# Tile 0 takes the norm's factor at the sums of MoE 1, smaller slice groups, low weight parts stored in DRAM, and a new hand-written order

## The chip, the cores and the metric

The kernel runs on one core of one Trainium2 chip. The metric is the device time of one execution in microseconds (us); the time of a kernel is the median of several executions. All four compute engines take part: TensorE (PE in the profile), VectorE (DVE), ScalarE (ACT) and GpSimd (POOL); SP only issues transfers. Each engine works through its own instructions strictly in the order in which the program lists them.

## The reference, cut to what matters

Three stages follow each other: a linear attention with a decay for each head, a gated MLP (MoE 1) on the normalised attention output, and a second gated MLP without a norm or a silu (MoE 2).

```python
# attention: B=2, H=8 heads, S=768 positions, D=64, blocks of 64 (the kernel uses chunks of 128)
intra = (q @ k.T) * Dmask              # decay lam**(i-j) inside a block
out   = intra @ v + (q * lam_pow) @ kv_state
kv_state = lam_block * kv_state + (k * rev_pow).T @ v
# x: 1536 tokens x 512
rms = sqrt(mean(x * x, -1) + 1e-6);  xn = x / rms * rms_g
g = xn @ w_gate;  y = (silu(g) * (xn @ w_val)) @ w_out     # MoE 1, d_ff = 1536
a = y @ w_a;      z = (a * (y @ w_b)) @ w_out2             # MoE 2, d_ff = 1536
```

## The kernel before

**Number format.** Every large product is done on numbers split into a high part and a low part (fp32r), as hi·hi + hi·lo + lo·hi. So a weight tile has a `whi` (a cast on ACT, L312, word `hi`) and a `wlo` (a subtraction on DVE, L317, word `lo`), and an activation tile has an `xhi` and an `xlo`. The weights arrive as integers of 64 bits and are turned into floats by two copies on ACT (L260, L264, word `c`) and seven operations on DVE (L282 to L301, word `k`) for each of 24 slices.

**Tiling.** The 1536 tokens are three tiles of 512 tokens. Each tile holds two chunks of 128 positions for both batches: tile 0 has chunks 0 and 1, tile 1 chunks 2 and 3, tile 2 chunks 4 and 5. d_ff is cut into 12 slices of 128 in each MoE. A plain step (`G` gate, `V` value, `O` output) takes one slice and one tile through 12 + 12 + 12 matmuls of 128x512. A pair step takes one slice and tiles 1 and 2 together through seven products `P` of 6 matmuls (a Strassen scheme on halves) and two outputs `Q` of 12. A pair slice needs its own sums of weight blocks (`ws` on DVE), their splits (`uh` on ACT, `ul` on DVE) and more element-wise work on both engines (`ps`, `pa`, `pm`, `sl`, `ph`, `pl`).

**Groups.** `GROUPS` cuts the slices: in MoE 1 slices 0 to 5 run plain for all three tiles and slices 6 to 11 run plain for tile 0 and as pairs for tiles 1 and 2. In MoE 2 all 12 slices are plain for tile 0 and pairs for the rest, in two groups. At the end of each group the sums in PSUM are added to SBUF (`E`, `e`: copies on ACT L572 for the first group, additions on DVE L574 for the others).

**Attention.** For chunk c and batch b: `S.b.c` scores (L358), `am` mask with the decay table `dt` on DVE (L369), `kd` and `qd` the decays of k and q on POOL (L337, L349), `U` the new state (L378), `I` and `X` the output (L393, L408). The state is decayed on POOL (`sd`, L418) and added to on DVE (`sa`, L428).

**The norm.** `sq` squares on ACT (L440); `rd` reduces four blocks of squares to one on DVE (L444); `R` sums over the partitions by matmuls with ones (L454), four of them where `rd` isn't done and one where it is; `ms` (DVE, L461), `rr` the power -1/2 on POOL (L468), `dg` a diagonal matrix (DVE, L473), `N` a matmul that spreads the factors over the partitions (L478), `nx` multiplies the attention output by factor and g (DVE, L484), `xh` and `xl` split it (ACT L492, DVE L498). In the kernel before `rd` is done for chunks 2 to 5. The gate of a tile can start when its two chunks have gone through all of this.

**Order.** Nothing is scheduled automatically. `PROGRAM` lists words such as `G.0` (gate of step 0) or `am.1.3.1` (mask, batch 1, chunk 3, half 1), and each word issues its instructions at once, so the list is the order on every engine. The transfers are words too: `l.i` a stage of weights of 512 KB on the SP queue (L234), `A` and `L` the pieces of q, k and v (L224), `Z` and `D` write the table of decays to DRAM and read it back spread over the partitions (L776, L753, L758). `W` issues dummy matmuls (L767) that keep PE active before there is work.

Of the kernel before, what the change touches and what calls it, by code (L numbers as in the profile page):

```python
# [38 lines left out]
GROUPS = [(0, 6), (6, 12)]  # L39

SLOTS, OUT_SLOTS = 7, 10

# [826 lines left out]
```

## Time and profile before

| | |
|---|---|
| time, median of 3 runs | 656.45 us (655.95 to 657.09) |
| profiled execution | 655.5 us, span 653.8 us |
| PE busy | 638.9 us (98%) |
| DVE busy | 520.1 us (80%) |
| ACT busy | 405.0 us (62%) |
| POOL busy | 39.7 us (6%) |
| mean granted clock of PE | 0.992 |

A profile comes from one execution. An engine's busy time is the time in which one of its instructions was running. A wait is named after what ended it: `[1.67 <-DVE nrm L473]` is idle time of 1.67 us that ended when that instruction of DVE did. The granted clock is 1.00 at 2.4 GHz and 0.50 at 1.2 GHz.

### The profile page before, as it was taken

The numbers are of one execution on the slowest core, as the hardware profiler recorded it, in microseconds if no ns is written. First come the engines' busy times: TensorE is split into PE (matmuls) and PEld (weight loads), VectorE is DVE, ScalarE is ACT, GpSimd is POOL, SyncE is SP. The second block draws the span as 40 slices with busy tenths as digits, with TensorE's granted clock in tenths as the row PEclk, the third lists the DMA queues.
The fourth block names the chain that finished last, engine by engine and source line by source line (L and its number), as shares of the span: only waits on it lengthen the run. The fifth ranks groups of instructions, "written<-read, shape, count | busy, mean of one in ns | idle before, by whom it ended". The sixth has DMA issues, their size and how long they took to land.

```text
span 653.8 us, 8719 instructions
## 1 busy us (share of the span) xinstructions
PE 638.9 (98%) x3304; PEld 517.5 (79%) x3306; DVE 520.1 (80%) x889; ACT 405.0 (62%) x642; POOL 39.7 (6%) x43
## 2 busy tenths in 40 slices
PE   9989999999999999999999999999999999999997
PEld 4767777787888888878887888888887888888876
DVE  4789999655579999889999988857968688776664
ACT  2878853332599884379888655665559873444441
POOL 1533122110000000000000000000000000000000
PEclk9969999999999999999999999999999999999999
DMA  8945641110036520013233120020023220100011
GB/s 262 378 156 188 226 161 65 65 65 1 4 127 194 162 96 1 1 36 126 66 99 127 64 65 1 0 66 33 1 96 97 67 63 1 65 1 0 2 64 65
DMA packets 16506, 54.84 MB, mean 84 GB/s; under 512 B 1864, under 2 KB 3408, under 8 KB 15440
## 3 DMA queue, kind: packets, MB, share of 16 engines
q1 hardware_dynamic: 15600, 47.99, 22.2%
q10 hardware_dynamic: 864, 6.29, 2.7%
q8 instruction: 26, 0.43, 0.3%
q14 instruction: 16, 0.13, 0.1%
HBM read 51.12 MB, written 3.15 MB: 83 GB/s over the span
## 4 chain that ended last, share of the span: by engine, by line
PE 86%; DVE 9%; DMA 2%; SPq 1%; ACT 1%; issue 0%; POOL 0%; ACTq 0%; DVEq 0%; POOLq 0%
PE acc L562 27%; PE at L706 15%; PE gv L706 11%; PE gv L514 6%; PE gv L518 6%; PE gv L515 5%; PE at L515 3%; PE at L514 3%; PE at L518 3%; DMA att<-att_dram 1%; DVE sums L574 1%; PE at L393 1%; PE at L358 1%; DVE wlo L317 1%; PE at L408 1%; DVE hh L301 1%
## 5 line engine op out<-in xcount | busy, mean ns | idle before, releaser
L260 ACT COPY hh<-stage 128x1024 uint8<-128x1024 uint8 x72 | 75.2, 1045 | 6.7 <-DMA stage<-w_dram 6.5
L514 PE MATMUL gv<-xhi,whi 128*128 128x512 f32 x192 | 76.7, 399 | 0.0
L317 DVE TENSOR_TENSOR wlo<-w,whi 128x512 fp32r<-128x512 f32 (+1 forms) x108 | 69.7, 654 | 7.8 <-ACT whi L312 7.8
L515 PE MATMUL gv<-xlo,whi 128*128 128x512 f32 x192 | 74.9, 390 | 0.0
L312 ACT CAST whi<-w 128x512 fp32r<-128x512 f32 (+1 forms) x108 | 60.5, 585 | 14.1 <-PE acc L562 5.6
L537 ACT CAST hhi<-s 128x512 fp32r<-128x512 f32 x36 | 22.4, 622 | 50.7 <-DVE s L533 49.1
L317 DVE TENSOR_TENSOR wlo<-o,whi 128x512 fp32r<-128x512 f32 x72 | 50.5, 705 | 3.5 <-ACT whi L312 3.4
L518 PE MATMUL gv<-xhi,wlo 128*128 128x512 f32 x192 | 51.6, 391 | 1.4 <-DVE wlo L317 1.4
L264 ACT COPY w<-stage 128x1024 uint16<-128x1024 uint16 x48 | 50.2, 1045 | 0.0
L312 ACT CAST whi<-o 128x512 fp32r<-128x512 f32 x72 | 44.2, 620 | 8.9 <-PE acc L562 4.3
L518 PEld LDWEIGHTS gv<-xhi,wlo 128*128 128x128 f32 x192 | 35.9, 188 | 9.7 <-DVE wlo L317 2.2
L562 PE MATMUL acc<-hlo,whi 128*128 128x512 f32 x144 | 42.1, 392 | 0.9 <-DVE hlo L541 0.6
L562 PE MATMUL acc<-whi,hlo 128*128 128x512 f32 x144 | 42.9, 391 | 0.0
L514 PEld LDWEIGHTS gv<-xhi,whi 128*128 128x128 f32 x192 | 36.1, 188 | 8.4 <-issue 0.9
L562 PE MATMUL acc<-hhi,whi 128*128 128x512 f32 x144 | 42.5, 395 | 0.2
L562 PE MATMUL acc<-whi,hhi 128*128 128x512 f32 x144 | 42.2, 392 | 0.1
L562 PE MATMUL acc<-wlo,hhi 128*128 128x512 f32 x144 | 41.8, 390 | 0.0
L515 PEld LDWEIGHTS gv<-xlo,whi 128*128 128x128 f32 x192 | 36.1, 188 | 7.0
L562 PE MATMUL acc<-hhi,wlo 128*128 128x512 f32 x144 | 41.5, 390 | 0.0
L706 PE MATMUL at<-T,whi 128*128 128x512 f32 x144 | 38.5, 389 | 0.0
L514 PE MATMUL at<-xhi,whi 128*128 128x512 f32 x96 | 37.3, 389 | 0.0
L515 PE MATMUL at<-xlo,whi 128*128 128x512 f32 x96 | 37.3, 389 | 0.0
(167 smaller groups left out, 1405.0 us busy)
## 6 DMA issues: line engine op xcount, KB each, us to landing
stage<-w_dram SPq DMA_DIRECT2D x72, 512.0 KB, 3.4
att<-att_dram ACTq DMA_DIRECT2D x6, 1024.0 KB, 4.8
att<-att_dram SPq DMA_DIRECT2D x6, 512.0 KB, 5.6
out_dram<-sums SPq DMA_DIRECT2D x12, 256.0 KB, 2.1
att<-att_dram SPq DMA_DIRECT2D x2, 1024.0 KB, 8.3
att<-att_dram SPq DMA_DIRECT2D x4, 256.0 KB, 9.6
dt<-ext_d SPq DMA_DIRECT2D x2, 256.0 KB, 4.7
p<-ext_d SPq DMA_DIRECT2D x2, 128.0 KB, 4.6
```

Of the source, the lines that this page charges most:

```text
L260: nc.scalar.copy(hh_t[i][:, into].bitcast(U8).rearrange("p (n e) -> p n e", e=2), st.rearrange("p (n e) -> p n e", e=8)[:, :, 3:5],)
L264: nc.scalar.copy(home(i, slice(place, place + 1)).bitcast(U16).rearrange("p (n e) -> p n e", e=2), st.bitcast(U16).rearrange("p (n e) -> p ...
L301: nc.vector.tensor_tensor(out=hh, in0=hh, in1=t, op=ALU.bitwise_or)
L312: nc.scalar.copy(whi[key], src)
L317: nc.vector.tensor_sub(wlo[key], src, whi[key].bitcast(F32))
L358: nc.tensor.matmul(ps[r][:, a * C : (a + 1) * C], lhsT=t[r * D : (r + 1) * D, 1, a * C : (a + 1) * C], rhs=t[r * D : (r + 1) * D, 0, a * C ...
L514: nc.tensor.matmul(ps, lhsT=w, rhs=xhi[t][:, k, :], start=k == 0, stop=False)
L515: nc.tensor.matmul(ps, lhsT=w, rhs=xlo[t][:, k, :], start=False, stop=False)
L518: nc.tensor.matmul(ps, lhsT=w, rhs=xhi[t][:, k, :], start=False, stop=k == KD - 1)
L537: nc.scalar.copy(h_t[g][0], s_t[g])
L562: nc.tensor.matmul(acc[j], lhsT=lhsT, rhs=rhs, start=first and n == 0, stop=last and n == 2)
L706: nc.tensor.matmul(ps, lhsT=w[:, k * 128 : (k + 1) * 128], rhs=x[:, k, :], start=first and n == 0, stop=n == len(todo) - 1, skip_group_che ...
```

## The change

1. `GROUPS` of MoE 1 becomes slices 0 to 2, 3 to 6 and 7 to 11. Only slices 0 to 2 run plain for all tiles; slices 3 to 11 are pairs for tiles 1 and 2. Plain steps go from 36 to 30 (the steps of tile 1 in slices 0 to 2 are `G.3` to `G.5`, those of tile 2 `G.6` to `G.8`, tile 0 goes on with `G.9`), pair slices from 18 to 21.
2. Tile 0 goes into MoE 1 as attention output times g, without the factor 1/rms. `xs` (ACT, four pieces of 128x128) and `xd` (DVE, four pieces) write its high and low part straight from PSUM. The factors are kept in a row `rv` (`rv`, ACT copy of the spread factors); the gate is multiplied by it ahead of the silu (`gs`, DVE, 12 steps), and the finished sums of MoE 1 are multiplied by it (`sr`, four DVE operations). `xg`, `nx`, `xh` and `xl` go away for chunks 0 and 1.
3. The state's decay leaves POOL (`sd` goes away); `sa` does decay and addition in four DVE operations of 128x64.
4. `rd` is done for chunks 4 and 5 only; `R` of chunks 2 and 3 is four matmuls again.
5. The low parts of slices 0 to 2 are computed once for tile 0, stored to DRAM (`ls`, 9 transfers of 256 KB) and loaded again for tiles 1 and 2 (`lr`, 18 transfers), all on the SP queue, in place of 18 subtractions.
6. `Z` and `D` are issued from ACT's queue. `l.0` is the first large transfer on SP's queue, with chunk 0 of q and k behind it.
7. The dummy matmuls go from 46 to 37, all ahead of `S.0.0`; before, 34 stood ahead of it and four times 3 between it and `G.0`.
8. The conversion of slice 1 is done in three parts (28 more `k` instructions). All words stand in a new order.

```diff
-GROUPS = [(0, 6), (6, 12)]
-SLOTS, OUT_SLOTS = 7, 10
-LAST_ATT = 11
+GROUPS = [[(0, 3), (3, 7), (7, 12)], [(0, 6), (6, 12)]]
+SLOTS, OUT_SLOTS = 7, 9
+def beside(i, t):
+    return i < GROUPS[0][0][1] and t < 2 or i < GROUPS[0][1][1] and t == 0
...
-    A.0.0.0 W.8.1 W.14 W.3.1 W.7.1 W.2.1 S.0.0 W.3.1 A.0.0.2 l.0 g Z A.1.0.0 A.1.0.2 D.0 D.1 A.0.1.0 A.1.1.3
+    W.14 W.8.1 W.7.1 W.2.1 l.0 A.1.0.0 A.1.1.0 A.0.1.0 A.0.0.0 A.0.0.2 A.1.1.3 A.1.0.2 g A.1.1.2 W.3.1 W.3.1 S.0.0
...
+    def lo_store(g, part):
+        nc.sync.dma_start(out=wlo_d[g * 3 + part], in_=wlo[g, part].bitcast(F32))
+    def lo_load(g, part):
+        wlo[g, part] = spool.tile([128, 512], F32R, tag="wlo", name="wlo")
+        nc.sync.dma_start(out=wlo[g, part].bitcast(F32), in_=wlo_d[steps[g][0] * 3 + part])
...
-    def state_decay(b, c):
-        nc.gpsimd.tensor_tensor(
-            out=st_t[b], in0=st_t[b], in1=p1[:, :, C - 1 : C].to_broadcast([128, NP, D]), op=ALU.mult
-        )
...
-            nc.vector.tensor_add(st_t[b], st_t[b], pu)
+            for a in range(NP):
+                nc.vector.scalar_tensor_tensor(
+                    out=st_t[b][:, a], in0=st_t[b][:, a], scalar=p1[:, a, C - 1 : C], in1=pu[:, a], op0=ALU.mult, op1=ALU.add
+                )
...
+    def att_hi(b, c):
+        hi = xtiles(0)[0]
+        for k in range(KD):
+            nc.scalar.mul(hi[:, k, c * 256 + b * C : c * 256 + (b + 1) * C], px_t[b, c][:, k * C : (k + 1) * C], g_sb[:, k, :])
+    def att_lo(b, c):
+        hi, lo = xtiles(0)
+        for k in range(KD):
+            some = (slice(None), k, slice(c * 256 + b * C, c * 256 + (b + 1) * C))
+            nc.vector.scalar_tensor_tensor(
+                out=lo[some], in0=px_t[b, c][:, k * C : (k + 1) * C], scalar=g_sb[:, k, :], in1=hi[some].bitcast(F32),
+                op0=ALU.mult, op1=ALU.subtract,
+            )
...
+    def factors(c):
+        nc.scalar.copy(rv[:, c * 256 : (c + 1) * 256], pr_t[c][:, 0:256])
...
+    def gate_factors(g):
+        s_t[g] = hpool.tile([128, 512], F32, tag="s", name="s")
+        nc.vector.tensor_tensor(out=s_t[g], in0=pg_t[g], in1=rv, op=ALU.mult)
...
+    def sum_factors(j):
+        nc.vector.tensor_tensor(out=sums[0][:, j, :], in0=sums[0][:, j, :], in1=rv, op=ALU.mult)
...
-                nc.sync.dma_start(
+                nc.scalar.dma_start(
                     out=dt[:, r],
...
-        "Z": lambda: nc.sync.dma_start(out=ext_d, in_=ext), "D": decay_tables,
+        "Z": lambda: nc.scalar.dma_start(out=ext_d, in_=ext), "D": decay_tables,
```

Three places show the new order. The first is PE ahead of the first gate `G.0`. Before, between the last matmuls with ones of chunk 1 (L454) and the gate (L514, here its first row) stand the spread of chunk 1's factors (L478), the scores of chunk 2 (L358, one of four pairs of rows shown) and the rest of chunk 2's batch 0:

```order
L454 MATMUL acc_445<-ones,sq 128x1 x4
L478 MATMUL at_472<-nrm,ones 128x128 x2
L358 MATMUL at_486<-att_2_293 128x128
L358 MATMUL at_487<-att_2_293 128x128
...
L378 MATMUL at_509<-att_2_293,kd 64x64 x8
L393 MATMUL at_518<-qd,st 64x128 x8
L408 MATMUL at_518<-am,att_2_293 64x128 x8
L514 MATMUL gv_535<-xhi_414,whi 128x512
```

After, with the names of the changed kernel's lines (L416 inter, L431 output of the attention, L514 spread, L490 matmuls with ones, L381 scores, L553 and L554 the gate, L401 state):

```order
L416 MATMUL acc_399<-spare,st 64x128 x8
L431 MATMUL acc_399<-am,att_1_158 64x128 x8
L514 MATMUL at_420<-nrm,ones 128x128 x2
L490 MATMUL acc_434<-ones,sq 128x1 x4
L381 MATMUL at_443<-att_2_441 128x128
L381 MATMUL at_444<-att_2_441 128x128
...
L553 MATMUL gv_470<-xhi_254,whi 128x512
L554 MATMUL gv_470<-xlo_255,whi 128x512
...
L401 MATMUL at_485<-att_2_441,kd 64x64 x8
L490 MATMUL acc_494<-ones,sq 128x1 x4
L553 MATMUL gv_531<-xhi_254,whi 128x512
```

The spread ahead of the gate is now chunk 0's; `U.0.2` (L401) and the matmuls of `R.1.1` (L490) stand behind the gate, and the spread of chunk 1, `I.0.2` and `X.0.2` behind the value `V.0`, which is the second L553 row.

The second is DVE in the changed kernel at the end of the stretch that leads to the normalisation of chunk 3 (L310 to L299 are the conversion of weights, L497 `ms`, L447 the state, L509 the diagonal, L523 `nx`, L392 the mask of the scores `S.0.4`):

```order
L310 TENSOR_SCALAR t<-t 128x1536
L295 TENSOR_SCALAR o_875<-o_875 128x512
L295 TENSOR_SCALAR w_831<-w_831 128x1024
L314 TENSOR_TENSOR hh<-hh,t 128x1536
L299 SCALAR_TENSOR_TENSOR o_875<-o_875,hh 128x512
L299 SCALAR_TENSOR_TENSOR w_831<-w_831,hh 128x1024
L497 TENSOR_SCALAR ms<-at_1043 128x1
L447 SCALAR_TENSOR_TENSOR st<-st,p_88,at_938 128x64 x4
L509 TENSOR_SCALAR nrm<-ident,rr 128x128 x2
L523 SCALAR_TENSOR_TENSOR spare<-spare,g_sb,at_1057 128x256 x4
```

All of slice 4's conversion stands ahead of `ms.1.3`, and the two words that the norm of chunk 3 needs next stand behind it. On PE the matmuls around it are these (L609 output, L490 `R.1.3`, L514 `N.3`, L381 `S.0.4`):

```order
L609 MATMUL acc_760<-hhi,wlo 128x512
L609 MATMUL acc_760<-hlo,whi 128x512
L490 MATMUL at_1043<-ones,sq 128x1 x4
L514 MATMUL at_1057<-nrm,ones 128x128 x2
L381 MATMUL at_1075<-att_4_833 128x128
L381 MATMUL at_1076<-att_4_833 128x128
```

Nothing else stands on PE between `R.1.3` and `N.3`, nor between `N.3` and `S.0.4`, and the gate of tile 1's first step comes behind the latter.

## Rows read from the trace of the kernel before

**Rows 1.** The page: busy time of PE, share of the span.

```profile
PE 638.9 (98%) x3304; PEld 517.5 (79%) x3306; DVE 520.1 (80%) x889; ACT 405.0 (62%) x642; POOL 39.7 (6%) x43
```

**Rows 2.** Windows by stage: PE, PEld, DVE, ACT, POOL busy, PEclk, DMA share.

```profile
11.40:44.40 33.00, 28.47 (x339) 23.32 (x340) 25.17 (x51) 21.89 (x30) 17.01 (x15) 0.84 0.84 294
31.00:33.70 2.70, 1.21 (x10) 1.03 (x9) 1.94 (x7) 2.45 (x4) 1.19 (x2) 0.94 0.75 293
33.70:43.30 9.60, 7.08 (x54) 5.88 (x56) 8.45 (x17) 7.11 (x9) 3.55 (x3) 0.50 0.55 182
...
44.40:100.00 55.60, 53.18 (x372) 42.19 (x371) 52.60 (x87) 42.40 (x61) 12.28 (x11) 1.00 0.54 182
...
100.00:120.00 20.00, 18.76 (x133) 15.03 (x131) 18.47 (x31) 9.16 (x17) 4.45 (x4) 1.00 0.08 34
120.00:275.00 155.00, 154.69 (x799) 127.16 (x798) 118.36 (x188) 93.27 (x146) 5.03 (x5) 1.00 0.23 75
275.00:390.00 115.00, 113.92 (x500) 93.17 (x499) 107.36 (x188) 92.02 (x146) 0.00 (x0) 1.00 0.26 83
```

**Rows 3.** Timeline of PE up to the first gate: start, duration, instruction, wait.

```profile
11.49 1.16 PE L358 MATMUL at<-att 64*128 64x128 f32 x16
...
18.11 0.69 PE L378 MATMUL acc<-att,kd 128*64 128x64 f32 x16
18.77 1.05 PE L454 MATMUL acc<-ones,sq 128*128 128x1 f32 x8
19.75 1.16 PE L358 MATMUL gv<-att 64*128 64x128 f32 x16
...
23.27 1.09 PE L408 MATMUL acc<-am,att 128*64 128x128 f32 x16 [0.35 <-DMA att<-att_dram]
...
26.50 0.81 PE L767 MATMUL gv<-warm 128*128 128x512 bf16 x3
27.24 0.69 PE L378 MATMUL acc<-att,spare 128*64 128x64 f32 x16
...
34.62 1.22 PE L478 MATMUL at<-nrm,ones 128*128 128x128 f32 x4 [1.67 <-DVE nrm L473]
...
37.69 2.05 PE L358 MATMUL at<-att 64*128 64x128 f32 x14 [1.11 <-DVE spare L484]
...
44.40 0.50 PE L514 MATMUL gv<-xhi,whi 128*128 128x512 f32 x1
```

**Rows 4.** Chain that ended last: start, duration, what.

```profile
33.23 1.03 POOL rr L468
...
35.88 1.67 DVE spare L484 x4
...
281.41 2.72 PE acc L562 x12
```

**Rows 5.** Timeline of DVE while it works without a gap.

```profile
61.52 0.69 DVE L282 TENSOR_SCALAR w<-w 128x1024 uint32<-128x1024 uint32 x1
62.12 0.55 DVE L295 TENSOR_SCALAR t<-t 128x1536 uint16<-128x1536 uint16 x1
62.59 0.69 DVE L317 TENSOR_TENSOR wlo<-w,whi 128x512 fp32r<-128x512 f32 x1
...
64.33 0.95 DVE L301 TENSOR_TENSOR hh<-hh,t 128x1536 uint16<-128x1536 uint16 x1
65.20 0.68 DVE L533 TENSOR_TENSOR s<-s,gv 128x512 f32<-128x512 f32 x1
65.80 0.68 DVE L286 SCALAR_TENSOR_TENSOR o<-o,hh 128x512 f32<-128x512 uint32 x1
66.40 1.22 DVE L286 SCALAR_TENSOR_TENSOR w<-w,hh 128x1024 f32<-128x1024 uint32 x1
67.53 0.48 DVE L473 TENSOR_SCALAR nrm<-ident,rr 128x128 f32<-128x128 f32 x2
```

**Rows 6.** DMA issues of the page: KB each, us from issue to landing.

```profile
out_dram<-sums SPq DMA_DIRECT2D x12, 256.0 KB, 2.1
```

More of the change, by code (lines that the diff above doesn't have):

```diff
@@ L201, in chain_kernel @@
     g_sb = cpool.tile([128, KD, 1], F32, tag="g_sb", name="g_sb")
+    rv = cpool.tile([128, 512], F32, tag="rv", name="rv")
     ones = cpool.tile([128, 128], F32, tag="ones", name="ones")
@@ L323, in split_lo @@
         unit_lo((g, part), third(steps[g][0], part))
+    wlo_d = dpool.tile([GROUPS[0][0][1] * 3, 128, 512], F32, tag="wlo_d", name="wlo_d")
+    def lo_store(g, part):
[3 more added lines that the diff above has]
+        nc.sync.dma_start(out=wlo[g, part].bitcast(F32), in_=wlo_d[steps[g][0] * 3 + part])
     a_t, kd_t, qd_t, st_t, ps_t, pu_t, px_t = {}, {}, {}, {}, {}, {}, {}
@@ L503, in chain_kernel @@
         (m * NF + f, t, f == lo, f == hi - 1)
-        for m in range(2) for lo, hi in GROUPS for t in range(1 if m or lo else len(TILES)) for f in range(lo, hi)
+        for m in range(2) for lo, hi in GROUPS[m] for t in range(1 if m or lo else len(TILES)) for f in range(lo, hi)
     ]
@@ L520, in gate @@
     def gate(g):
-        pg_t[g] = bank("at0" if g > LAST_ATT and g % 2 else "gv0")
+        pg_t[g] = bank("at0" if g % 2 and not beside(*steps[g][:2]) else "gv0")
         proj(pg_t[g], g, 0)
     def value(g):
-        pv_t[g] = bank("at1" if g > LAST_ATT and g % 2 else "gv1")
+        pv_t[g] = bank("at1" if g % 2 and not beside(*steps[g][:2]) else "gv1")
         proj(pv_t[g], g, 1)
+    def gate_factors(g):
+        s_t[g] = hpool.tile([128, 512], F32, tag="s", name="s")
+        nc.vector.tensor_tensor(out=s_t[g], in0=pg_t[g], in1=rv, op=ALU.mult)
     def silu(g):
-        s_t[g] = hpool.tile([128, 512], F32, tag="s", name="s")
-        nc.scalar.activation(s_t[g], pg_t[g], AF.Silu if steps[g][0] < NF else AF.Copy)
+        i, t, _, _ = steps[g]
+        if i < NF and t == 0:
+            nc.scalar.activation(s_t[g], s_t[g], AF.Silu)
+        else:
+            s_t[g] = hpool.tile([128, 512], F32, tag="s", name="s")
+            nc.scalar.activation(s_t[g], pg_t[g], AF.Silu if i < NF else AF.Copy)
     def gated(g):
@@ L744, in pair_out @@
         f = i % NF
-        first, last = f in [x for x, _ in GROUPS], f + 1 in [x for _, x in GROUPS]
+        first, last = (f + n in [x[n] for x in GROUPS[i // NF]] for n in range(2))
         out_part(i, (i, "u", 3 + t), h_t[i, t], first, last, slice(a, b))
@@ L757, in decay_tables @@
             else:
-                nc.sync.dma_start(
+                nc.scalar.dma_start(
                     out=p1[r * D : (r + 1) * D],
```

262 lines of the change are left out of this document (134 added, 128 removed).

## The prediction

> **What bounds the kernel now.** I read the page first: PE is busy for 98% of the span, at a mean clock of 0.992 [rows 1]. So time comes only from three places: matmuls that go away, the few microseconds in which PE waits, and the stretch at half clock. The windows say where these lie [rows 2]. From 11.4 to 44.4 us PE is busy 28.47 of 33.00 us and its clock is 0.84. From 44.4 to 120 us it loses 2.42 + 1.24 us. From 120 to 390 us it loses 0.31 + 1.08 us, and DVE is busy 76% and then 93% of the time. The tail behind 390 us keeps the same work in both kernels and I leave it out. Then I read the timeline of PE up to the first gate [rows 3]: the gate `G.0` starts at 44.40 us, 32.9 us after the first scores. Its waits are a queue of dependences of the norm: `N.1` waits 1.67 us for the diagonal, which waits for POOL's `rr`, 1.03 us, and `S.0.2` waits 1.11 us for the four `nx` of DVE, 1.67 us, because it needs their PSUM bank [rows 3, 4]. While PE did 1.21 us of work in 2.7 us the clock fell, and from 33.7 to 43.3 us it stood at 0.50, which is 1.2 GHz, with 7.08 us of PE work inside [rows 2]: half of that, 3.5 us, is the price of the clock.
>
> **Term 1, the way to the first gate.** Of the 32.9 us, 4.5 are idle, 3.5 are the half clock, and four times three dummies take about 0.74 each time (26.50 to 27.24 less what the next needs), 3.0 in all [rows 2, 3]. That leaves 21.9 us of work at full clock. The change moves `U.0.2`, `I.0.2`, `X.0.2`, `R.1.1` and `N.1` behind the gate. `U` takes 0.66 and `R` 0.98 (their starts to the next start), `X` and `I`, sixteen short matmuls each, about 1.0 (1.09 less the overlap of about 0.08 that other neighbours show), and `N` about 0.5 at full clock [rows 3]: 4.1 us. So 17.8 us stand ahead of the gate. The first scores start later, since 37 dummies stand ahead of them and not 34: I add 3 x 0.3 and put them at 12.4. Without the `nx`, `xh` and `xl` of two chunks the gate waits only for the last `xs` and `xd`, and `N.0`, `R.0.1` and `S.0.2` (0.5 + 0.98 + 1.1) lie beside these; I allow 1.0 of waiting. The table's transfers `Z` and `D` now wait on ACT's queue, with the first weight copies `c.0.1` behind them; these have some 20 us until `G.0` needs their result, so I cost it at nothing, and if that cover fails the gate is late by the rest. `G.0` then starts near 31.2 in place of 44.4, 13.2 earlier, of which 4.1 are paid behind it: **-9.1**. Bounds: -10.1 without any wait; -4 if the table `dt` comes later behind the larger loads or the clock falls here again.
>
> **Term 2, matmuls.** Six plain steps fewer are 6 x 36 matmuls of 512 columns, three pair slices more are 3 x 42 products and 3 x 24 outputs: -216 + 198 = -18. Twelve take 2.72 us [rows 4], so **-4.1**. `rd` away for four (b, c) turns one matmul into four: four take 0.98 [rows 3], one at most a quarter, so 0.73 or more are lost each time; with 0.15 for a lone one it is 0.83: **+3.3**, lower bound 2.9.
>
> **Term 3, DVE around chunk 3.** The order shows `S.1.3`, and behind it on PE `N.2`, `V.2`, `O.1`, `R.0.3`, `U.1.3`, `I.1.3`, `X.1.3`, `O.2` and `R.1.3`: 0.5 + 3 x 2.72 + 2 x 0.98 + 0.66 + 2 x 1.0 = 13.3 us [rows 3, 4]. From `am.1.3.1` to `ms.1.3` DVE must do, by the distance of starts in its gapless stretch [rows 5]: eight operations of 128x512 at 0.60 (two masks, `mu`, `hl`, two `lo`, two `xl`), 4.8; of the conversion two of L286 on `o` at 0.60 and two on `w` at 1.13, 3.5; two of L282 on `w` at 0.60 and two on `o` at about 0.34, 1.9; two of L301 at 0.87 and four others at 0.47, 3.6; four `nx`, 1.7 [rows 4]; two `ms`, 0.2. That is 15.7, so DVE reaches `ms.1.3` about 2.4 us after PE is through with `R.1.3`. What follows took from 33.23 to 37.55 before: `rr`, `dg`, `N`, four `nx`, with 0.5 us of PE work inside [rows 3, 4]: 3.8 us idle. Together some 6 us of waiting, a part of it already at `V.2` for its last `lo`, and I add 0.8 for small waits at `S.1.2`. Before, 44.4 to 120 us lost 3.7 [rows 2]; so **+3.1**, bounds 0 (DVE ahead, the stretch like before) and +6.
>
> The clock: before, it fell when PE had idled about half of 2.7 us [rows 2]. Here it would idle some 5 of 6 us, so a fall is likelier than not. It costs nothing if the gate of tile 1 comes at once at full clock, 3.5 if it lasts as before. I take **+1.2**. The Trainium skill (TensorE: Matmul & The Clock Gate, section HAM oscillation) says that such a drop is paid again after every gap that is long enough. The trace agrees for the one at 33.7 us, and the 1.24 us lost between 100 and 120 us left the clock at 1.00 [rows 2], so not every wait pays.
>
> **Term 4, the middle.** What DVE gains and loses, at the durations of rows 5 (0.69 for 128x512): 36 `lo` fewer -25, 18 `ul` +12, 12 `ws` of 256 columns +5, nine `pa`, six `pm`, six `pl` +14, six `mu` and `hl` fewer -8, eight more additions of sums +5, 12 `gs` and 4 `sr` +11, 28 more conversion pieces +3, `nx`, `xl`, `rd` fewer -11, `xd` (16 of 128x128 at 0.20 to 0.29, [rows 5] L473) +4, `sa` +2 to +4 (four pieces at 0.10 to 0.24 for one at 0.41): about +13 us. All lies ahead of 390 us, in which DVE then is busy 335 of 374 us from 11.4 us on, 90%, against 322 of 378.6, 85%, before [rows 2]. From 275 to 390 us it was at 93% and cost PE 1.08 us [rows 2]. So that much load can be hidden, nearly: **+1.0**, bounds 0 and +9 (below). POOL loses 8 `sd`, which are no term. A store and a load of low parts take about as long as the 2.1 us of a 256 KB transfer each [rows 6] and are ordered at least ten microseconds ahead of their use; uncovered, a load late would cost 2.1 each.
>
> The Trainium skill (VectorE: DVE Perf Modes, section The TRN2 errata) speaks against the change: each DVE instruction pays a fixed cost beside its elements, so four pieces of 64 columns cost more than one of 256. By the cycles that it states, an estimate, `sa` rises by 0.36 us each, 2.9 in all. The row of 0.48 for two of 128x128 agrees with such a cost [rows 5]. It lies inside the bounds of Term 4.
>
> **Sum.** -9.1 - 4.1 + 3.3 + 3.1 + 1.2 + 1.0 = -4.6, against the profiled execution's 655.5: 650.9. The median of the runs is 0.95 above that execution, so I say 651.8. The term that is most likely too dark is Term 3, and (a) is what is left if it is.
>
> **Rivals.**
> (a) The hand count of Term 3 is too dark: DVE has run ahead, `N.3` waits no more than `N.1` did before and the clock stays up. Then Terms 3 and 4 shrink to +1 together: 655.5 - 9.1 - 4.1 + 3.3 + 1 = 646.6, median 647.5. For it speaks that no wait up to the first gate is longer than 1.67 us [rows 3]; against it the order, in which `ms.1.3` stands behind a whole conversion. 0.22.
> (b) Slower: DVE becomes the bound of the pairs of MoE 1. From the first pair `P.3` to the plain steps `G.13` to `G.17` and the next pairs DVE has, counted from the order and rows 5, as much work as PE (about 165 us each), where before the same kind of stretch had 131 against 141. If DVE can only be busy for the 93% that it reached from 275 to 390 us [rows 2], 165 us take 177, 11 us more than Term 4 has: 655.5 - 4.6 + 11 = 661.9, median 662.8; a little over half of it is enough for slower. It decides from a DVE that is busy over 95% for 100 us with PE waiting for `wlo`, `hlo` or `usum`. Against it: from 61.5 to 67.5 us DVE ran with no gap at all [rows 5], in a window in which PE lost 2.4 of 55.6 us [rows 2]. 0.12.
> (c) The start gives less: tables and pieces of q, k and v compete with the weight stage that now goes first, and `G.0` starts near 36. Then Term 1 is -4: 656.0, median 656.9, no change. Against it: chunk 1's pieces, which PE waited for at 23.27 us [rows 3], are issued earlier, for the queue no longer waits for the table. 0.10.
> (d) The fall at chunk 3 costs all of 3.5 and comes twice, around `S.1.2` too: +5.8, median 657.6: 0.06. The forecast itself, 649 to 654, has 0.50.
>
> **Chances.** A measurement of this kernel can tell a change of 0.2%, 1.3 us, from none: same is 655.1 to 657.8. Faster holds the forecast, (a) and a part of (c): 0.78. Same holds most of (c) and (d): 0.10. Slower is (b): 0.12. The range reaches from the better bound of (a), 645.5, to 657.5, which leaves out (b) and the far end of (a).
>
> **What would show it.** `G.0` near 31 us, with a clock at 1.00 from 12 to 31; if it stands at 36 or later, Term 1 is wrong. PE's waits for DVE at `N.3` and `S.0.4` of 3 to 6 us together, and whether the clock stands at 0.50 behind them; if neither, Term 3 is wrong. PE's records of L490 at 1.0 us each for chunks 2 and 3. In the windows from the first pair on: PE's idle time of 1 to 3 us up to the point where MoE 1 ends; ten or more is (b). I would be wrong altogether if PE's busy time did not fall by some 6 to 8 us: 4.1 - 3.3 of matmuls, 3.0 of dummies and 3.5 of half clock, less a new fall.

## The result: slower by 0.9%

The changed kernel takes 661.94 us (median of 4 runs, 661.81 to 664.7) against 656.49 us before: a ratio of 1.0093, 95% interval 1.0065 to 1.012. The forecast was 651.8 us with a range of 645.5 to 657.5. The profiled execution took 664.7 us with a span of 662.5, some 3 us more than its median; its mean clock is 0.979, against 0.983 to 0.986 in the others. I make the sums with its own numbers.

The first view is the page of the changed kernel: the busy times, and the clock in 40 slices of the span.

```profile
PE 640.3 (97%) x3303; PEld 522.1 (79%) x3303; DVE 532.7 (80%) x968; ACT 416.0 (63%) x664; POOL 32.2 (5%) x35
...
PEclk9779986999999999999999999999999999999999
```

PE is busy 1.4 us longer than before [rows 1], although 18 large matmuls and 9 dummies have gone. The clock shows why: it is low in the slices up to 110 us. The windows place it (columns as in [rows 2]).

```profile
11.67:42.45 30.78, 22.45 (x270) 19.55 (x269) 19.65 (x51) 15.40 (x33) 12.12 (x11) 0.82 0.74 240
17.90:24.40 6.50, 5.63 (x52) 4.68 (x54) 3.49 (x8) 1.63 (x5) 3.49 (x3) 0.50 0.79 235
38.40:45.10 6.70, 6.70 (x32) 5.95 (x33) 5.55 (x19) 5.12 (x8) 0.00 (x0) 0.50 0.10 39
44.40:120.00 75.60, 66.86 (x506) 53.43 (x505) 64.53 (x130) 53.40 (x76) 14.15 (x11) 0.90 0.73 244
...
86.00:90.00 4.00, 4.00 (x12) 3.10 (x12) 4.00 (x7) 2.02 (x4) 0.00 (x0) 0.57 0.66 224
100.00:110.00 10.00, 8.28 (x29) 6.18 (x29) 8.80 (x14) 7.21 (x11) 2.83 (x2) 0.50 0.55 185
120.00:275.00 155.00, 155.00 (x801) 126.79 (x800) 135.18 (x239) 105.53 (x168) 4.99 (x4) 1.00 0.27 85
275.00:390.00 115.00, 115.00 (x509) 95.21 (x508) 109.85 (x194) 90.76 (x141) 0.00 (x0) 1.00 0.28 87
```

From 120 to 390 us nothing is lost: PE is busy 155.00 of 155 and 115.00 of 115 us, though DVE is at 87% and 96%, more than before [rows 2]. Behind 390 us PE idles 3.6 us, where it had idled 3.9. So all of the loss is ahead of 120 us. Before there was one stretch at half clock; now there are four. The timeline of PE (start, duration, instruction, wait) shows the waits ahead of them.

```profile
11.67 1.16 PE L381 MATMUL at<-att 64*128 64x128 f32 x16
12.66 1.06 PE L381 MATMUL gv<-att 64*128 64x128 f32 x16
...
18.00 0.69 PE L431 MATMUL acc<-am,att 128*64 128x128 f32 x2 [4.28 <-DVE am L392]
19.45 1.97 PE L431 MATMUL acc<-am,att 128*64 128x128 f32 x14 [0.76 <-DVE am L392]
...
37.27 0.49 PE L514 MATMUL at<-nrm,ones 128*128 128x128 f32 x2 [2.27 <-DVE nrm L509]
38.29 0.72 PE L514 MATMUL at<-nrm,ones 128*128 128x128 f32 x2 [0.53 <-DVE nrm L509]
...
42.45 0.79 PE L553 MATMUL gv<-xhi,whi 128*128 128x512 f32 x1
...
84.80 1.20 PE L557 MATMUL gv<-xhi,wlo 128*128 128x512 f32 x4 [2.27 <-DVE wlo L330]
...
98.92 0.71 PE L514 MATMUL at<-nrm,ones 128*128 128x128 f32 x4 [1.41 <-DVE nrm L509]
...
101.55 2.04 PE L381 MATMUL at<-att 64*128 64x128 f32 x14 [1.43 <-DVE spare L523]
```

The first product of a mask (L431) waits 4.28 us and then 0.76 us; the chain says for what (start, duration, what):

```profile
4.13 5.53 DMA ext_d<-nrm
...
9.69 0.44 ACTq L803
...
10.17 8.45 DMA dt<-ext_d
```

The second half of the decay table lands at 18.6 us. In the kernel before, the write ahead of it took 3.81 us, and the table's two transfers were issued 1.7 us earlier and took 4.7 us each. The chain there, and the view of the table's tile:

```profile
4.13 3.81 DMA ext_d<-nrm
...
L753 SPq DMA_DIRECT2D dt<-ext_d x2: 387/447/507, 8.0 to 8.5; - x2
...
DMA to landing us min/median/max: 4.7/4.7/4.7
```

Its first product of a mask waited for nothing that the trace shows and ran between the scores and `U`. So `G.0` starts at 42.45 us, only 1.95 earlier than before [rows 3], where 13.2 had been forecast.

The second stop ahead of `G.0` is `N.0`, which waits 2.27 + 0.53 us for DVE. DVE was not late for lack of input; it was slow. The timelines of DVE and, below it, of POOL:

```profile
35.02 0.99 DVE L308 TENSOR_SCALAR t<-t 128x512 uint16<-128x512 uint16 x1
35.94 2.30 DVE L509 TENSOR_SCALAR nrm<-ident,rr 128x128 f32<-128x128 f32 x2
```

```profile
34.61 1.26 POOL L372 TENSOR_TENSOR qd<-att,p 128x512 f32<-128x512 f32 x1
35.83 1.31 POOL L372 TENSOR_TENSOR spare<-att,p 128x512 f32<-128x512 f32 x1
37.10 1.05 POOL L360 TENSOR_TENSOR spare<-att,dt 128x512 f32<-128x512 f32 x1
```

The two diagonals took 2.30 us, in place of 0.48 [rows 5], and the small conversion step ahead of them 0.99 us, where the same step takes 0.29 a few rows earlier, at 30.05 us. Each of the three DVE instructions ends within 0.2 us of the end of one of POOL's.

### The profile page after: what moved, and what is told of

It is laid out like the page before. It is cut to its first block, busy times and chain, and to the rows that moved or that the text cites. A ratio compares the mean times of both kernels' runs of the same rounds, so it can differ in the third digit from the quotient of the medians.

```text
span 662.5 us, 8890 instructions
## 1 busy us (share of the span) xinstructions
PE 640.3 (97%) x3303; PEld 522.1 (79%) x3303; DVE 532.7 (80%) x968; ACT 416.0 (63%) x664; POOL 32.2 (5%) x35
## 4 chain that ended last, share of the span: by engine, by line
PE 91%; DVE 4%; DMA 2%; ACT 2%; issue 1%; ACTq 0%; DVEq 0%
PE acc L609 29%; PE at L756 18%; PE gv L756 13%; PE gv L557 6%; PE gv L553 6%; PE gv L554 5%; PE at L553 3%; PE at L554 3%; PE at L557 3%; PE at L381 2%; DMA dt<-ext_d 1%; PE at L431 1%; PE at L416 1%; DMA ext_d<-nrm 1%; PE acc L431 1%
## 5 line engine op out<-in xcount | busy, mean ns | idle before, releaser
L553 PE MATMUL gv<-xhi,whi 128*128 128x512 f32 x160 | 66.2, 414 | 0.0
L330 DVE TENSOR_TENSOR wlo<-w,whi 128x512 fp32r<-128x512 f32 (+1 forms) x90 | 56.2, 627 | 11.1 <-ACT whi L325 11.1
L554 PE MATMUL gv<-xlo,whi 128*128 128x512 f32 x160 | 64.4, 402 | 0.3 <-DVE xlo L537 0.3
L330 DVE TENSOR_TENSOR wlo<-o,whi 128x512 fp32r<-128x512 f32 x66 | 44.7, 684 | 6.4 <-ACT whi L325 6.4
L557 PE MATMUL gv<-xhi,wlo 128*128 128x512 f32 x160 | 43.9, 397 | 3.5 <-DVE wlo L330 3.5
L756 PE MATMUL at<-T,whi 128*128 128x512 f32 x172 | 46.0, 389 | 0.0
L609 PE MATMUL acc<-hhi,whi 128*128 128x512 f32 x144 | 44.2, 399 | 0.0
L609 PE MATMUL acc<-hlo,whi 128*128 128x512 f32 x144 | 43.9, 392 | 0.0
L609 PE MATMUL acc<-hhi,wlo 128*128 128x512 f32 x144 | 43.8, 396 | 0.0
L609 PE MATMUL acc<-whi,hlo 128*128 128x512 f32 x144 | 43.2, 390 | 0.0
L609 PE MATMUL acc<-whi,hhi 128*128 128x512 f32 x144 | 41.7, 390 | 0.0
L609 PE MATMUL acc<-wlo,hhi 128*128 128x512 f32 x144 | 41.5, 389 | 0.0
L557 PEld LDWEIGHTS gv<-xhi,wlo 128*128 128x128 f32 x160 | 30.5, 191 | 10.7 <-DVE wlo L330 4.3
L553 PEld LDWEIGHTS gv<-xhi,whi 128*128 128x128 f32 x160 | 31.3, 196 | 7.9 <-issue 1.3
L756 PEld LDWEIGHTS at<-T,whi 128*128 128x128 f32 x172 | 32.3, 188 | 6.7
L554 PEld LDWEIGHTS gv<-xlo,whi 128*128 128x128 f32 x160 | 31.2, 195 | 7.1 <-DVE xlo L537 1.0
L330 DVE TENSOR_TENSOR wlo<-wsum,whi 128x512 fp32r<-128x512 f32 x42 | 28.6, 685 | 10.1 <-ACT whi L325 10.0
L584 ACT CAST hhi<-s 128x512 fp32r<-128x512 f32 x30 | 18.6, 621 | 25.3 <-DVE s L580 18.7
```

What stands on the lines that cost most here:

```text
L330: nc.vector.tensor_sub(wlo[key], src, whi[key].bitcast(F32))
L553: nc.tensor.matmul(ps, lhsT=w, rhs=xhi[t][:, k, :], start=k == 0, stop=False)
L554: nc.tensor.matmul(ps, lhsT=w, rhs=xlo[t][:, k, :], start=False, stop=False)
L557: nc.tensor.matmul(ps, lhsT=w, rhs=xhi[t][:, k, :], start=False, stop=k == KD - 1)
L584: nc.scalar.copy(h_t[g][0], s_t[g])
L609: nc.tensor.matmul(acc[j], lhsT=lhsT, rhs=rhs, start=first and n == 0, stop=last and n == 2)
```

## The experiments

Two theories stood at first. A: the table lands late, because it now shares the DMA engines with loads that no longer wait behind it, and the wait brings the clock down. B: the norm of chunk 0 holds the gate, since DVE's diagonal is slow while POOL works. A third, C, was the forecast's own: DVE's order around chunk 3. All ratios are against the kernel before on the same chip. In the edits a long line of words is cut to the stretch around the change.

**E1, e1_tables_sp.** The tables return to SP's queue, in the order of before.

```diff
-    W.14 W.8.1 W.7.1 W.2.1 l.0 A.1.0.0 A.1.1.0 A.0.1.0 A.0.0.0 A.0.0.2 A.1.1.3 A.1.0.2 g A.1.1.2 W.3.1 W.3.1 S.0.0
-    A.0.1.3 l.1 A.0.1.2 l.3 S.1.0 Z D.0 D.1 c.0.1
+    W.14 W.8.1 W.7.1 W.2.1 A.0.0.0 A.0.0.2 l.0 g Z A.1.0.0 W.3.1 W.3.1 S.0.0
+    A.1.0.2 D.0 D.1 A.0.1.0 A.1.1.3 A.1.1.0 l.1 A.0.1.2 A.1.1.2 l.3 S.1.0 A.0.1.3 c.0.1
-                nc.scalar.dma_start(
+                nc.sync.dma_start(
```

> The changed kernel with the start of the SP queue as in the kernel before: Z and D issued from SP, the loads of chunk 1 behind them. Theory A (the decay table lands late because it shares the DMA engines with all loads that were issued at once, and its wait of 5 us ahead of the first masked product brings the clock down): the table lands near 13 us, the first L431 starts near 15 us in place of 18.0, the clock holds from 17 to 25 us, G.0 comes 5 to 8 us earlier, time 654 to 657 us. Rival B (the gate is held by the norm of chunk 0, whose diagonal is slow on DVE): the start moves, but the wait at N.0 grows by what is won, time 660 to 662 us.

Measured: 659.32 us, ratio 1.0034 (1.0014 to 1.0054). The table lands as in the kernel before, and the first product starts at 13.80 us. But the pieces of chunk 1 now come late, as they did before, and take a part of it back, on PE:

```profile
22.44 0.69 PE L401 MATMUL acc<-att,spare 128*64 128x64 f32 x16 [2.49 <-DMA att<-att_dram]
...
25.47 1.12 PE L401 MATMUL acc<-att,kd 128*64 128x64 f32 x16 [1.36 <-POOL kd L360]
...
39.55 0.79 PE L553 MATMUL gv<-xhi,whi 128*128 128x512 f32 x1
```

`G.0` comes 2.9 us earlier than in the changed kernel, less than the 5 to 8 of A, and the time lies between the two expectations. A holds for the table; in this order the pieces of chunk 1 are pushed back for it.

**E2, e2_dummies.** Dummies in the wait for the table.

```diff
-    am.1.0.0 am.1.0.1 kd.0.0 X.0.0
+    am.1.0.0 am.1.0.1 kd.0.0 W.18 X.0.0
```

> The changed kernel with 18 dummy matmuls (about 4 us) ahead of the first masked product, in the wait for the decay table. Theory A: the wait stays, the clock holds from 17 to 25 us and the 2.8 us that the half clock costs there come back: about 659 us. Rival: the clock falls there anyway, or the time won is lost again at N.0: 661 to 662 us.

Measured: 657.05 us, ratio 1.0009 (0.9985 to 1.0034). The wait is as long as it was (the first product starts at 18.68 us), the clock holds up to 36 us, and `G.0` is at 39.45 us, 3.0 earlier, about the 2.8 us expected. The median is 4.9 us lower. The rest lies behind `G.0`, where the fall of the clock at chunk 3 is shorter in this trace; the run does not show that the dummies shortened it.

**E3, e3_dg_act.** All diagonals on ACT.

```diff
-            nc.vector.tensor_scalar_mul(dg_t[c][:, b, :], ident, rr_t[c][:, b : b + 1])
+            nc.scalar.mul(dg_t[c][:, b, :], ident, rr_t[c][:, b : b + 1])
```

> The changed kernel with the two diagonal matrices of each norm made on ACT in place of DVE. Theory B (DVE's two instructions for the diagonal of chunk 0 took 2.3 us in place of 0.48 because POOL was at work on kd and qd at the same time): N.0 waits 1 us or less in place of 2.8, the clock holds from 38 to 45 us, 4 to 5 us less: about 657 us. Rival (the diagonal is late for its input, rr, and not slow): no change, 661 to 662 us.

Measured: 662.23 us, ratio 1.0085 (1.006 to 1.011): no gain in the time. The trace shows two halves of opposite sign. On PE:

```profile
34.28 0.71 PE L514 MATMUL at<-nrm,ones 128*128 128x128 f32 x4
...
98.77 1.22 PE L514 MATMUL at<-nrm,ones 128*128 128x128 f32 x4 [4.80 <-ACT nrm L509]
```

`N.0` waits for nothing, the clock does not fall behind it, and `G.0` is at 37.59 us, 4.9 earlier. But `N.3` waits 4.80 us, where it had waited 1.41, since ACT has its diagonal behind a row of copies of weights and sums. Most of what was won at chunk 0 was lost at chunk 3. The time alone would have refuted B.

**E4, e4_k4_late.** The conversion of slice 4 behind chunk 3's norm.

```diff
-    lo.2.2 xl.2.1 k.4.3 k.4.2 k.4.5 k.4.6 I.1.3 X.1.3 L.1.4 O.2 sq.1.3 E.2.0 xg.1.3 c.5.2 E.2.2 l.17 c.6.0 hi.5.0
+    lo.2.2 xl.2.1 I.1.3 X.1.3 L.1.4 O.2 sq.1.3 E.2.0 xg.1.3 c.5.2 E.2.2 l.17 hi.5.0
-    nx.3.0 xh.3.0 xl.3.0 xh.3.1 k.5.0 xl.3.1 c.6.1
+    nx.3.0 xh.3.0 k.4.3 xl.3.0 xh.3.1 k.4.2 xl.3.1 k.4.5 k.4.6 k.5.0 c.6.0 c.6.1
```

> The changed kernel with the last four conversion steps of slice 4 (six DVE instructions, 4 us) behind the normalisation of chunk 3 in place of ahead of ms.1.3, and the copy c.6.0 behind them. Theory C (DVE is late at chunk 3, and the two waits of 1.4 us there bring the clock down for 10 us): the wait ahead of N.3 falls below 1.4 us, the clock holds from 100 to 110 us or falls for less, time 656 to 658 us. Rival: R.1.3, the chain ms, rr, dg, N.3, nx is the wait and not DVE's queue, so the clock falls the same and the conversions come late for slice 4: 661 to 663 us.

Measured: 664.6 us, ratio 1.0126 (1.0102 to 1.0151), above both expectations. `N.3` waits 1.40 us as before the edit. C falls: at `ms.1.3` DVE was ahead, not behind. In the trace of the changed kernel it stands idle there and waits for PE:

```profile
97.55 0.16 DVE L497 TENSOR_SCALAR ms<-at 128x1 f32<-128x1 f32 x1 [0.88 <-PE at L490]
```

PE had already waited for DVE at `V.2` (2.27 us, above), and the 1.4 us at `N.3` are the bare chain of `ms`, `rr`, `dg`.

What makes `V.2` wait is in good part POOL again. DVE and, below it, POOL ahead of that wait in the changed kernel:

```profile
81.83 1.46 DVE L306 TENSOR_SCALAR t<-hh 128x1536 uint16<-128x1536 uint16 x1
...
83.60 1.15 DVE L330 TENSOR_TENSOR wlo<-w,whi 128x512 fp32r<-128x512 f32 x1
```

```profile
80.91 1.96 POOL L372 TENSOR_TENSOR qd<-att,p 128x512 f32<-128x512 f32 x1 [5.99 <-DMA att<-att_dram]
82.83 1.37 POOL L360 TENSOR_TENSOR kd<-att,dt 128x512 f32<-128x512 f32 x1
```

In the trace of E6, where both DVE instructions began with POOL idle, they take 0.56 and 0.68 us, 1.4 less together, and `V.2` waits 0.90 us in place of 2.27. In the trace of E4 two other DVE instructions ahead of `V.2` (L295) are stretched by 1.7 us together, and the wait is 2.61. No run here moves POOL's words at this place.

**E5, e5_pool_late.** POOL's decays of chunk 2 behind the factors of chunk 1.

```diff
-    kd.0.2 U.0.2 R.1.1 ms.1.1 k.1.5.1
+    R.1.1 ms.1.1 rr.1 kd.0.2 k.1.5.1
-    qd.0.2 ls.0.1 l.7 lr.3.0 lr.3.1 l.6 V.0 qd.1.2 kd.1.2 rr.1 dg.1
+    qd.0.2 ls.0.1 l.7 lr.3.0 lr.3.1 l.6 V.0 U.0.2 qd.1.2 kd.1.2 dg.1
```

> The changed kernel with POOL's four decays of chunk 2 (kd and qd) behind the factors of chunk 1 in its order, so that POOL is idle while DVE makes the diagonal of chunk 0; U.0.2 moves behind V.0. Theory B (DVE's small copies wait while POOL runs): the two L509 of chunk 0 take 0.5 us in place of 2.3, N.0 waits about 1 us in place of 2.8, the clock holds from 38 to 45 us or falls for less; G.0 4 to 5 us earlier; time 656 to 658 us unless U.0.2 or I.0.2 then wait for POOL. Rival (the diagonal is slow by itself): L509 takes as long, time 661 to 663 us.

Measured: 663.9 us (659.91 to 667.32), ratio 1.0105 (1.0068 to 1.0141), above the range of either expectation. DVE's timeline confirms the mechanism twice, first with POOL idle, then with POOL at work on the four decays from 43.34 to 48.0 us; POOL's last three are below:

```profile
34.99 0.28 DVE L308 TENSOR_SCALAR t<-t 128x512 uint16<-128x512 uint16 x1
35.19 0.48 DVE L509 TENSOR_SCALAR nrm<-ident,rr 128x128 f32<-128x128 f32 x2
...
44.58 1.25 DVE L312 TENSOR_SCALAR hh<-hh 128x512 uint16<-128x512 uint16 x1
45.75 1.35 DVE L308 TENSOR_SCALAR t<-t 128x512 uint16<-128x512 uint16 x1
47.02 1.27 DVE L509 TENSOR_SCALAR nrm<-ident,rr 128x128 f32<-128x128 f32 x2
```

```profile
44.36 1.32 POOL L372 TENSOR_TENSOR qd<-att,p 128x512 f32<-128x512 f32 x1
45.64 1.31 POOL L372 TENSOR_TENSOR spare<-att,p 128x512 f32<-128x512 f32 x1
46.91 1.10 POOL L360 TENSOR_TENSOR spare<-att,dt 128x512 f32<-128x512 f32 x1
```

The diagonal of chunk 0 takes 0.48 us, `G.0` is at 38.20 us. The collision has moved to the diagonal of chunk 1: `N.1` waits 2.72 us and the clock is at half from 48 to 59 us. That two conversion steps of 0.28 us take 1.25 and 1.35 us, and a pair of diagonals 1.27 in place of 0.48, are the rows to remember: each of the three ends 0.1 to 0.3 us behind the end of one of POOL's. The Trainium skill (SBUF — State Buffer, section SBUF: two separate sides) says that DVE, in its two-port modes or with two inputs in SBUF, and GpSimd share a pair of ports that one of them holds for a whole instruction, while the other is blocked. These rows agree: each of the three lasts about as long as one POOL instruction, 1.10 to 1.32 us.

**E6, e6_warm3.** Dummies at chunk 3's norm.

```diff
-    rr.3 sa.1.3 dg.3 N.3 nx.3.2
+    rr.3 sa.1.3 dg.3 W.7.1 N.3 W.8.1 nx.3.2
```

> The changed kernel with 7 dummy matmuls ahead of N.3 and 8 behind it, in the two waits of 1.4 us that chunk 3's norm leaves on PE. Theory D (the waits themselves are small and the clock that falls there for 10 us is what costs): the clock holds from 100 to 110 us, 3 to 5 us less: 657 to 659 us. Rival (the fall comes from the waits before, at 83 us): no gain, 661 to 663 us.

Measured: 659.42 us (655.98 to 665.03), ratio 1.0047 (1.0017 to 1.0077). The clock stays up from 92 to 126 us. The time is 2.5 us below the changed kernel's. A shorter fall remains from 88 to 92 us, behind a wait of 1.06 us for `ms.0.3`.

**E7, e7_all.** E2 and E6 together, the diagonal on ACT for chunk 0 alone, and one subtraction earlier.

```diff
-            nc.vector.tensor_scalar_mul(dg_t[c][:, b, :], ident, rr_t[c][:, b : b + 1])
+            (nc.scalar.mul if c == 0 else nc.vector.tensor_scalar_mul)(dg_t[c][:, b, :], ident, rr_t[c][:, b : b + 1])
-    S.1.3 am.1.3.1 k.3.2 k.3.5 N.2 c.4.0 c.4.2 k.4.0 nx.2.1 lo.2.1
+    S.1.3 lo.2.1 am.1.3.1 k.3.2 k.3.5 N.2 c.4.0 c.4.2 k.4.0 nx.2.1
```

> The changed kernel with the 18 dummies in the wait for the table, the diagonal of chunk 0 alone on ACT, the dummies at chunk 3's norm, and the subtraction lo.2.1 ahead of the conversion of slice 3. If the start's wait, the slow diagonal and the falls of the clock are all that stands between the forecast and the measured time: 661.9 - 4.9 (as e2) - 4 (as the start of e3) - 4 = 649 us. If they share one cause or the next wait takes their place: 654 to 657 us.

Measured: 653.93 us, ratio 0.9953 (0.9934 to 0.9973): faster than before. `G.0` is at 35.73 us and the clock at 1.00 from 12 to 36 us:

```profile
12.00:36.00 24.00, 23.03 (x290) 17.90 (x289) 16.49 (x47) 14.80 (x33) 12.40 (x11) 1.00 0.88 302
```

The time lies between the two expectations, just below the second: the repairs overlap, and some 4 of these 23 us are dummies.

**E8, e8_before_act.** The one edit in the kernel before: tables from ACT's queue.

```diff
-                nc.sync.dma_start(
+                nc.scalar.dma_start(
                     out=dt[:, r],
-        "Z": lambda: nc.sync.dma_start(out=ext_d, in_=ext), "D": decay_tables,
+        "Z": lambda: nc.scalar.dma_start(out=ext_d, in_=ext), "D": decay_tables,
```

> The kernel before with Z and D issued from ACT's queue, its loads in the same order on SP. Theory A: the loads of chunk 1 no longer wait behind the table, share the engines with it, and the table lands 2 to 4 us later than 13.2 us; the first product of the mask is late by as much, chunk 1's pieces come earlier than 23.1 us, so the time is 655 to 659 us. Rival (a transfer from ACT's queue is slow by itself): the same delay of 5 us as in the changed kernel and 659 to 662 us.

Measured: 663.77 us, ratio 1.0114 (1.0087 to 1.0141). This part alone costs the kernel before 7.3 us, more than the whole change. The chain and the first gate there:

```profile
4.09 5.30 DMA ext_d<-nrm
...
9.89 10.25 DMA dt<-ext_d
```

```profile
54.15 0.50 PE L514 MATMUL gv<-xhi,whi 128*128 128x512 f32 x1
```

`G.0` is 9.75 us later than in [rows 3], and table and time are later than either expectation. The loads are in the same order, but SP no longer stops for the table, and the loads behind it run beside it: five loads of q, k and v are issued on SP by 10.7 us, where before two were, and the next came from 10.39 us on, behind the reads of the table. Whether that or ACT's queue makes the table late, this run doesn't tell; E13 does.

**E13, e13_dt_act.** The kernel before with only the table `dt` issued from ACT; its write and its other half `p` stay on SP, so SP still stops.

```diff
-                nc.sync.dma_start(
+                nc.scalar.dma_start(
                     out=dt[:, r],
```

> The kernel before with the two transfers of the decay table dt alone issued from ACT's queue; the table's write to DRAM and its other half p stay on SP, so SP's queue still stops for the write and the loads of chunk 1 are held back as before. Theory A (the freed loads make the table late): dt is issued near 8.0 us, takes 4.5 to 6 us, G.0 stays within 1.5 us of 44.4 and the time is 655 to 658 us. Rival (ACT's queue is slow by itself): dt takes 8 us or more, G.0 comes near 50 us or later, 660 to 664 us.

Measured: 658.55 us, ratio 1.0026 (1.0006 to 1.0046). The chain there:

```profile
4.10 3.75 DMA ext_d<-nrm
...
8.37 6.14 DMA dt<-ext_d
```

The table's write takes 3.75 us as before, where E8 has 5.30, and `dt` 6.14, where the kernel before has 4.7 and E8 10.25. It lands at 14.5 us, 1.3 later than before, and in E8 at 20.1. So of the 6.9 us by which E8's table is late, ACT's queue accounts for at most 1.3, and the freed loads for the rest. Not all of the 1.3 need be the queue's: SP issues `p` and the loads behind it 1.1 us earlier here than before, beside the table. It is mostly A. `G.0` comes at 47.50 us, 3.1 later and more than the 1.5 that A allowed: PE waits 1.29 us for the table, and at `N.1` 2.58 + 0.22 us where it had waited 1.67 [rows 3]. This second wait is POOL's: the two diagonals of chunk 1 take 2.21 us at 35.21 us, under POOL instructions that run from 35.06 to 37.33 us, and had taken 0.48 before.

**E9, e9_tables_all.** The tables at their old place as in E1, with the weight stages `l.1` and `l.3` behind the pieces of chunk 1; the diagonal of chunk 0 on ACT; E6; and two words earlier on DVE.

```diff
-    A.1.0.2 D.0 D.1 A.0.1.0 A.1.1.3 A.1.1.0 l.1 A.0.1.2 A.1.1.2 l.3 S.1.0 A.0.1.3 c.0.1
+    A.1.0.2 D.0 D.1 A.0.1.0 A.1.1.3 A.1.1.0 A.0.1.2 A.1.1.2 A.0.1.3 l.1 l.3 S.1.0 c.0.1
```

(against E1)

> The changed kernel with the tables back on SP's queue at their old place and the weight stages l.1 and l.3 behind the pieces of chunk 1; the diagonal of chunk 0 on ACT; the dummies at chunk 3's norm; lo.2.1 ahead of the conversion of slice 3 and ms.0.3 ahead of hl.2. No dummies stand in for the table. If the late table was a wait that can be taken away and not only covered, G.0 starts 3 us or more earlier than in the run with all repairs and covered table (36.0 us there), time 648 to 652 us. Rival (the pieces of chunk 1 take the table's place as the thing that is late): G.0 at 36 us or later, time 653 to 657 us.

Measured: 650.38 us (648.24 to 651.2), ratio 0.9903 (0.9877 to 0.9929): the best of all, 5.4 us less than before on the same chip, and 11.6 less than the changed kernel. `G.0` is 2.0 us earlier than in E7, where 3 or more had been expected. No dummy stands in for the table. PE:

```profile
30.93 0.71 PE L514 MATMUL at<-nrm,ones 128*128 128x128 f32 x4
...
33.72 0.50 PE L553 MATMUL gv<-xhi,whi 128*128 128x512 f32 x1
```

**E10, e10_rd23.** E7 with DVE's sum of squares for chunks 2 and 3 again.

```diff
-    ls.1.1 R.0.2
+    ls.1.1 rd.0.2 R.0.2
```

(and so for each of the four `R` of chunks 2 and 3)

> The repaired kernel of e7 with rd (DVE's sum of four blocks) for chunks 2 and 3 as before. Its matmuls with ones go from four to one: 3.3 us of PE less, four DVE instructions of 1.09 us more. If DVE's order binds the stretch of chunks 2 and 3, nothing is won: 653 to 656 us; if PE does, 650 to 651 us.

Measured: 659.77 us, ratio 1.0053 (1.0033 to 1.0073), 5.8 us more than E7. The view of PE's waits (us in total, times, longest):

```profile
PE at L490 <- DVE nrm L480: 8.6, 3, 4.9
```

So the part of the change that I charged with 3.3 us of PE is worth more than it costs, in this order: it takes PE off DVE's queue.

**E11, e11_no_store.** E7 without the store and the loads of low parts; each low part is computed right behind its high part.

```diff
-    N.0 rv.0 hi.3.0 xd.1.1
+    N.0 rv.0 hi.3.0 lo.3.0 xd.1.1
...
-    ls.0.1 l.7 lr.3.0 lr.3.1 l.6
+    l.7 l.6
```

(and so for all 18 parts of steps 3 to 8 and all 27 transfers)

> The repaired kernel of e7 with the 18 low parts of slices 0 to 2 for tiles 1 and 2 computed on DVE again, each right behind its high part, without the 27 transfers. DVE has 18 x 0.6 = 11 us more between 70 and 150 us, where it is busy about 85%. Theory: most of it is hidden behind PE, which is the bound there: 654 to 658 us; rival (the store is what keeps DVE from being the bound): 660 us or more.

Measured: 676.62 us, ratio 1.0314 (1.029 to 1.0338). That is 22.7 us more than E7, and 18 subtractions are only 11 us of DVE's time. A row of DVE shows a part of the rest:

```profile
99.85 0.69 DVE L330 TENSOR_TENSOR wlo<-w,whi 128x512 fp32r<-128x512 f32 x1 [6.19 <-ACT whi L325]
```

DVE stands 6.19 us at one of the added words, with the norm of chunk 3 behind it, and PE then waits 4.25 us at `N.3`. The run shows what a badly placed word costs, and not what the store is worth; that stays open.

**E12, e12_ms03.** E7 with two more words moved on DVE (`lo.2.1` behind the mask, `ms.0.3` ahead of `hl.2`).

```diff
-    S.1.3 lo.2.1 am.1.3.1 k.3.2
+    S.1.3 am.1.3.1 lo.2.1 k.3.2
...
-    k.4.1 hh.2 hl.2 xl.2.0 xh.2.1
+    k.4.1 hh.2 xh.2.1
...
-    c.5.1 ms.0.3
-    lo.2.2 xl.2.1
+    c.5.1 ms.0.3
+    hl.2 xl.2.0 lo.2.2 xl.2.1
```

> The repaired kernel of e7 with lo.2.1 behind am.1.3.1 and with ms.0.3 ahead of hl.2 and xl.2.0 on DVE. In e7 PE waited 1.4 us for that mask and 1.7 us for ms.0.3, and the clock fell once, from 80 to 86 us. If these two places in DVE's order are the cause: 2 to 4 us less, 650 to 652 us, the clock at 1.00 throughout; if the waits move to the next instruction: 653 to 655 us.

Measured: 653.8 us, ratio 0.9946 (0.9923 to 0.997), the same as E7. `I.1.3` still waits 1.87 us for `ms.0.3`. DVE's timeline says why: DVE has no gap from 71.6 to 86 us, `R.0.3` is through on PE at about 79.3 us, and the words of conversion ahead of `ms.0.3` (`k.4.4`, `k.3.6`, `k.4.1`) run up to 81.5 us.

## Why the prediction was wrong, point by point

**What bounds the kernel** was read rightly: time can come only from matmuls, waits and the clock ahead of 120 us, and all of the difference lies there.

**Term 1 failed**, and with it the forecast. I put `G.0` at 31.2 us and allowed 1.0 us of waiting; it was 42.45, 11.3 later, against a miss of 10.1 in the time. The step that failed is the sentence that costs the move of `Z` and `D` at nothing because the weight copies behind them on ACT have 20 us. I named what was queued behind them, and not what the table itself had to share. Rival (c) said it and was given 0.10 and 36 us. Of the 30.8 us from the first scores to `G.0`, 8.3 were idle (30.78 less 22.45 busy), and 5.63 + 4.05 us of work ran at 1.2 GHz (17.9 to 24.4, and 38.4 to 42.45), which costs half, 4.8. The 17.8 us of work were right: 30.8 less 8.3 and 4.8 is 17.7. Where I had nothing, the runs show three causes one by one (E2, E3, E5, E8 and E13): the late table, the diagonal slowed by POOL, and the clock behind each.

The diagonal was a second hole in this term. I priced DVE's work by rows without looking at what POOL did at that time. The trace of before had the pattern in it: a subtraction of 1.14 us at 29.05 us and a conversion step of 1.55 us at 26.01 us, both next to others of 0.68 and under a running POOL instruction.

**Term 2** came as counted: 2,484 to 2,466 large matmuls in the order, and `R` of chunks 2 and 3 at 0.94 to 0.95 us each in the timeline. E10 shows that the 3.3 us of `R` are well spent in this order.

**Term 3** had the place right, the size too small and the cause in part wrong. From 44.4 to 120 us PE lost 8.7 us against 3.7 before [rows 2], +5.1 where I had +3.1. What I had as DVE's lag at `ms.1.3` came at `V.2`, 2.27 us for a low part (E4), and 1.4 of it is DVE stretched by POOL, which I had at nothing; `N.3` and `S.0.4` waited 1.41 + 1.43 us, where I had 3.8. The clock, for which I took 1.2 us with a bound of 3.5, cost 4.1 from 100 to 110 us (half of 8.28), 1.7 from 86 to 90, and 1.3 behind `G.0`, 7.1 in all in the profiled execution. Its median execution is 2.8 us shorter at a higher mean clock, so the usual price is smaller. The Trainium skill (TensorE: Matmul & The Clock Gate, section HAM oscillation) describes a loop in which each long wait brings the clock down again, so that the cost is paid many times and not once. That fits better than my bound, which had one fall there (rival (d) had two): here it was paid at four places, behind waits of 4.28, 2.27 + 0.53, 2.27 and 1.41 + 1.43 us.

**Term 4** was on the safe side. I had +1.0 and a rival (b) of +11 that DVE becomes the bound. DVE was at 96% from 275 to 390 us and PE lost nothing there, where before it had lost 1.08 at 93% [rows 2]. Rival (b) gave the right sign by a mechanism that didn't occur; that is luck. The count of DVE's work came out: it is busy 12.6 us more than before, the stretched rows included, where I had 13. The four pieces of `sa` take 0.44 us more than the one operation did, where I had estimated 0.36. A store of a low part took 5.7 us and a load 2.8 (medians), more than my 2.1; PE waited for none.

From `G.0` to the end the spans give 620.05 us against 609.4 before, +10.65, of which 4.1 are the moved work: +6.5. The pieces make -4.1 + 3.3 + 5.1 + 7.1 - 1.4 (the waits of the middle that are gone) = +10.0. Some 3.5 us of gain are not resolved; a busy PE can hide short waits, and I didn't try to separate them.

**What was right about the change itself.** With the repairs of E9 it takes 650.4 us, 1.0% less than the kernel before and close to the forecast of 651.8; but by another sum, since 33.7 us for `G.0` is not 31.2. No run gives the kernel before the same care (dummies in a wait, a diagonal on ACT), so how much of the 1.0% is the change's own stays open.

## What to carry to other kernels

When a queue stops for something, ask what its stop was holding back: freeing it let everything behind it run beside the transfer that was urgent (E8, 7.3 us; 2.4 in E13, where SP still stops). Price a wait together with the stretch of half clock behind it: in the changed kernel waits of 5.0, 2.8 and 2.8 us (for the table, at `N.0`, at chunk 3) were followed by falls that cost 2.8, 3.3 and 4.1. When a row is used as a price for a DVE instruction, look at what POOL does beside it. And a time that doesn't move is no verdict on a cause: E3 won 4.9 us and lost most of them 60 us later.
